# One transpose transfer for two heads' exponentials, a bfloat16 identity, more engine options and a new order in an attention and two-layer MoE kernel

## The chip, the cores and the metric

The kernel runs on one core of a Trainium2 chip. The metric is the device time of one launch in microseconds (us), lower is better. A profile of one execution of the kernel before is read below; its stretches are in us from the span's start.

## What is computed

The reference runs attention with a position bias and then two feed-forward layers, here called MoE 1 and MoE 2, on the result (batch 4, 8 heads, 576 positions, head width 64, model width 512, inner width 2048):

```python
scores = scale * np.matmul(q, k.transpose(0, 1, 3, 2))
x = (psi_rel / psi_i)[..., None]          # log1p distances
h = np.maximum(x @ w1 + b1, 0.0)
bias = h @ w2                             # one bias matrix for each head
scores = scores + bias.transpose(2, 0, 1)[None, :, :, :]
scores = scores - np.max(scores, axis=-1, keepdims=True)
attn = np.exp(scores)
attn = attn / (np.sum(attn, axis=-1, keepdims=True) + 1e-09)
attn_out = np.matmul(attn, v)             # then (tokens 2304, width 512)
r = np.maximum(x @ moe_w_in, 0.0)
x = (s * (r * r) + b) @ moe_w_out         # MoE 1
h = x @ moe2_w_in
out = (h - np.tanh(h)) @ moe2_w_out       # MoE 2
```

## The kernel before, in words

All products are made in half precision with a high and a low part (three products high-high, high-low, low-high), so most values are split into `hi` (a copy in float16) and `lo` (the remainder).

**The planner.** No order is written out by hand. Each piece of work is a task (`sc.add`) with the engines that may run it and a cost on each. While the program is built, class `Schedule` walks through the tasks in simulated time: of those that can start first it emits the one with the lowest priority number, which is a due time plus an entry of the table `SHIFT`. `COST` multiplies the costs by kind of task and engine, `XFER` the time and landing delay of transfers, `ENGINE` narrows the engines of a kind in one stage. Each engine then executes its own instructions in the emitted order. All transfers are issued from one queue, SP's, in order too. Buffers are rings: an instance of a ring with n slots can start only when the instance n places before it has been used up.

**The bias.** `bias_tasks` makes 36 strips Q: four hidden tiles (`hid`, on DVE, ACT, or POOL for Q < `QG`), a matmul (`pb`), two scaling copies into a tile of the ring `et` (`out`, on ACT or DVE), and a store to `btd` in DRAM. The heads load their bias rows `bi` from there.

**A unit.** 144 units stand for 144 heads' blocks of 128 query rows (with 64 rows left over, two heads share one). `unit_rest` does for each: add the bias and take the maximum (`ttr`, DVE, L1073), add a constant to the maximum (`mx_add`, L1081), the exponential into `e` (`ex`, ACT, L1087), its float16 copy (`hi`, L1097 on DVE or L1099 on ACT) and its remainder (`lo_a`, `lo_b`, L1104 on POOL or DVE) into one tile of the ring `hl` (3 slots), a transpose transfer of that tile's nine blocks of 128 columns into a tile of the ring `et` (4 slots, shared with the bias strips; L1119), and 14 matmuls with the values (`pv`, L1132 and L1138). Scores come from `qk` (L1041) into two PSUM slots `s`, which the exponential frees.

```python
def tr(_):
    nc.sync.dma_start_transpose(
        out=put(et, row_tile("et", F16).rearrange("p (n r) -> p n r", r=128)), in_=hl.tile
    )
t_tr[u] = sc.add({SP: (1.25, 1.4)}, tr, t_lo, d + 5 - 500, [et], [hl])
```

**The rest.** Four units make a group; `x_tasks` scales it, splits it (`xh`) and transposes it (L1217, L1220). MoE 1 runs in nine blocks of 256 tokens between the units: `ph` matmuls (L1573), `relu` and `square` on ACT (L1586, L1591), `hi` and `lo`, `po` matmuls (L1645). Its weights arrive as 64-bit numbers and are converted by three DVE passes (L1253, L1256, L1259), bounded by `norm_max` (a matmul `pm` with a 128 x 128 identity, L1341) and split (`w1_split`). When the last unit is done, `turn` changes the buffers, the weights of MoE 2 are converted and split, mostly on DVE, and 18 half blocks run through `in_product` (L2038, results `pa`, `pb`, copied by `copy`, L2057) and `out_product` (L2166, `acc`).

Of the kernel before, what the change touches and what calls it, by code (L numbers as in the profile page):

```python
# [31 lines left out]
COST = {
    "u.ex@act": 0.848, "u.hi@act": 0.904, "bias.lambda@act": 1.1, "f.relu@act": 0.952, "f.square@act": 1.15,
    "x.lambda@act": 1.2, "w.lambda@act": 1.13, "scan.sq@act": 1.17, "bias.out@act": 1.0315, "f.out@act": 1.1149,
    "w.square@act": 1.07, "k.hi@act": 1.15, "s.lambda@act": 1.09, "q.hi@act": 1.2, "v.hi@act": 1.14,
    "u.ttr@dve": 0.84944, "f.hi@dve": 1.152216, "u.hi@dve": 0.87312, "s.in_done@dve": 1.1143, "scan.add@dve":
    0.8125, "f.lambda@dve": 1.174, "s.out_done@dve": 1.662, "u.lo@pool": 0.9991, "f.lo@pool": 0.782085,
    "bias.lambda@pool": 1.0466, "u.qk@pe": 0.885, "u.pv@pe": 0.97, "u.tr@sp": 1.04, "x.lambda@sp": 1.083,
    "q.fn@sp": 1.36, "J.c@dve": 1.2701, "J.fn@dve": 1.12, "L.lambda@dve": 1.0069, "L.square@act": 0.919,
    "P.wsum@dve": 1.0042, "X.scales@dve": 0.7943, "X.sums@dve": 1.21, "X.xsum@dve": 1.1245, "bias.lambda@dve":  # L40
    1.0453, "bias.out@dve": 1.179, "f.norm@dve": 1.2446, "f.out@dve": 1.0696, "f.scales@dve": 0.4404,
    "k.hi@dve": 1.1296, "k.lambda@dve": 1.047, "q.hi@dve": 1.1098, "s.lambda@dve": 1.0224, "scan.lambda@dve":
    0.857, "v.hi@dve": 1.738, "v.lambda@dve": 1.0251, "w.lambda@dve": 0.993, ".begin@dve": 0.784, ".lambda@dve":
    1.116, "L.scales@dve": 0.961, "L.sums@dve": 0.868, "X.lambda@act": 1.021, "X.lambda@dve": 1.023,
    "q.lambda@dve": 1.026, "w.scale_out@dve": 0.859, "u.lo@act": 0.97, "u.lo_a@act": 0.97, "u.lo_b@act": 0.97,
    "u.lo@dve": 0.97, "u.lo_a@dve": 0.97, "u.lo_b@dve": 0.97, "u.lo_a@pool": 0.97, "u.lo_b@pool": 0.97,
    "f.lo@act": 0.85, "f.lo@dve": 0.85, "f.hi@act": 1.04, "f.hi@pool": 1.04, "u.hi@pool": 0.8, "u.ex@dve": 0.8,
    "u.ex@pool": 0.8, "u.ttr@act": 0.8, "u.ttr@pool": 0.8,
}
# [2277 lines left out]
```

## Time and the profile before

| | us |
|---|---|
| median of three runs | 1053.27 (1051.8 to 1054.85) |
| the profiled execution | 1057.96 |
| its span, first to last instruction | 1056.2 |
| PE busy in the span | 964.1 |
| DVE busy | 881.6 |
| ACT busy | 667.5 |
| POOL busy | 250.1 |

The profiled execution took 1.76 us more than its span and 4.69 us more than the median of the runs. The units run from about 40 to 572 us, the last block of MoE 1 ends at about 704 us, and the products of MoE 2 fill the rest. PE is TensorE's matmuls, PEld its weight loads, DVE is VectorE, ACT ScalarE, POOL GpSimd, SPq the queue from which transfers are issued. The granted clock (PEclk) is a share of the full 2.4 GHz; the other level, 1.2 GHz, shows as 0.5.

### The profile page before, as it was taken

To read this page: it belongs to the slowest core of one execution; us is meant where nothing else is said; L and a number is where in the kernel's file an instruction comes from. 1 tells how busy PE (TensorE), PEld (TensorE's weight loads), DVE (VectorE), ACT (ScalarE), POOL (GpSimd) and SP (SyncE) were. 2 spreads that over 40 slices of the span, in tenths; PEclk is the share of its full clock that TensorE was granted. 3 is DMA by queue.
4 is the path that set the end of the run, shared out by engine and by line. 5 is a ranking of instruction groups with operands and counts; after the bars stand their busy time and mean duration, and the time that the engine had idled before them with its cause. 6 is when DMAs were issued, how large, how long until landed. Compare 5 with 4: busy or idle time off the path is not lost.

```text
span 1056.2 us, 32450 instructions
## 1 busy us (share of the span) xinstructions
PE 964.1 (91%) x13486; PEld 833.2 (79%) x13486; DVE 881.6 (83%) x1918; ACT 667.5 (63%) x1307; POOL 250.1 (24%) x319
## 2 busy tenths in 40 slices
PE   5676678999988999999997999988999999999998
PEld 3233356778767788788886888878999999999998
DVE  6999899876568677786774889999999999999885
ACT  4797659749767565776853687766554555464452
POOL 6146437247542334455511000000000000000000
PEclk9767679899999999999999999998999999999999
DMA  9969995899999879999896904410001100100000
GB/s 341 398 227 216 311 236 119 184 200 252 245 197 230 168 179 176 201 188 207 171 180 104 397 21 138 148 36 12 32 23 32 52 23 22 42 22 23 22 22 22
DMA packets 261444, 153.66 MB, mean 145 GB/s; under 512 B 197680, under 2 KB 229552, under 8 KB 261296
## 3 DMA queue, kind: packets, MB, share of 16 engines
q1 hardware_dynamic: 261296, 151.59, 59.1%
q8 instruction: 105, 1.72, 0.7%
q14 instruction: 43, 0.35, 0.1%
HBM read 84.03 MB, written 20.33 MB: 99 GB/s over the span
## 4 chain that ended last, share of the span: by engine, by line
PE 43%; DVE 9%; ACT 3%; DMA 2%; issue 2%; POOL 1%; SPq 0%; DVEq 0%; ACTq 0%; POOLq 0%
PE acc L2166 14%; PE pa L2038 9%; PE pb L2038 7%; PE po L1645 5%; PE ph L1573 4%; PE po L2166 2%; DMA et<-hl 2%; DVE w2big L1852 2%; DVE w2big L618 1%; PE sp L1041 1%; DVE w1big L618 1%; ACT e L1087 1%; POOL hl L1104 1%; PE xp L1132 1%; DVE hr L1603 1%
## 5 line engine op out<-in xcount | busy, mean ns | idle before, releaser
L1645 PE MATMUL po<-hr,w1big 128*128 128x256 f16 x1728 | 202.9, 274 | 3.6 <-ACT x L1664 2.7
L1104 POOL TENSOR_TENSOR hl<-e,hl 128x64 f16<-128x64 f32 (+1 forms) x200 | 160.2, 818 | 184.9 <-ACT hl L1099 107.2
L1573 PEld LDWEIGHTS <-w1big 128*128 128x128 f16 x1728 | 166.9, 99 | 31.5 <-issue 10.6
L1645 PEld LDWEIGHTS <-w1big 128*128 128x128 f16 x1728 | 165.5, 98 | 26.5 <-issue 7.1
L2038 PEld LDWEIGHTS <-w2big 128*128 128x128 f16 x3024 | 175.2, 99 | 2.2 <-issue 2.1
L2166 PEld LDWEIGHTS <-w1big 128*128 128x128 f16 x3024 | 172.8, 98 | 0.0
L1087 ACT ACTIVATE e<-sp,mx 128x576 f32<-128x576 f32 x144 | 105.6, 735 | 70.3 <-POOL mx L1081 34.3
L1073 DVE CUSTOM_DVE_ANT_0 sp<-sp,bi 128x576 f32<-128x576 f32 x144 | 107.0, 772 | 20.2 <-PE sp L1041 16.2
L1573 PE MATMUL ph<-xt_own,w1big 128*128 128x256 f16 x960 | 113.1, 274 | 3.0 <-ACT r L1586 2.2
L1041 PE MATMUL sp<-ks,qs 64*128 64x288 f16 (+1 forms) x960 | 84.2, 296 | 25.8 <-ACT e L1087 24.8
L1573 PE MATMUL ph<-w1big 128*128 128x256 f16 x768 | 91.2, 276 | 3.3 <-ACT r L1586 2.6
L1041 PEld LDWEIGHTS <-qs 64*128 64x128 f16 (+1 forms) x960 | 48.7, 99 | 53.0 <-issue 42.2
L1132 PEld LDWEIGHTS <-et 128*128 128x128 f16 (+1 forms) x1440 | 54.7, 104 | 41.2 <-issue 21.5
L1132 PE MATMUL xp<-vp,et 128*128 128x64 f16 (+1 forms) x1440 | 65.4, 199 | 19.1 <-DMA et<-hl 11.7
L2166 PE MATMUL acc<-hr,w1big 128*128 128x128 f16 x1296 | 79.9, 219 | 0.0
L1099 ACT ACTIVATE hl<-e 128x576 f16<-128x576 f32 x96 | 64.7, 678 | 23.1 <-DMA et<-hl 20.2
L2166 PE MATMUL acc<-w2big,w1big 128*128 128x128 f16 x1296 | 79.0, 219 | 0.0
L1104 DVE TENSOR_TENSOR hl<-e,hl 128x512 f16<-128x512 f32 (+1 forms) x88 | 48.8, 572 | 15.9 <-ACT hl L1099 13.0
L2038 PE MATMUL pa<-w1big,w2big 128*128 128x128 f16 x960 | 59.9, 219 | 1.7 <-ACT w2big L2057 0.9
L1586 ACT ACTIVATE r<-ph 128x512 f32<-128x512 f32 x72 | 42.3, 590 | 25.8 <-PE ph L1573 21.3
L1591 ACT ACTIVATE r<-r,sq 128x512 f32<-128x512 f32 x72 | 51.2, 718 | 0.9
L2074 ACT ACTIVATE w1big<-w1big 128x512 f32<-128x512 f32 x34 | 21.3, 630 | 45.6 <-DVE w1big L2064 33.4
(229 smaller groups left out, 1757.7 us busy)
## 6 DMA issues: line engine op xcount, KB each, us to landing
bi<-btd SPq DMA_DIRECT2D x64, 288.0 KB, 4.1
w1big<-in_wout SPq DMA_DIRECT2D x12, 1024.0 KB, 6.0
btd<-et SPq DMA_DIRECT2D x36, 295.5 KB, 3.7
w1big<-in_win SPq DMA_DIRECT2D x8, 1024.0 KB, 9.7
w2big<-in_win SPq DMA_DIRECT2D x8, 1024.0 KB, 13.1
x2d<-x SPq DMA_DIRECT2D x36, 128.0 KB, 3.1
w1big<-x2d SPq DMA_DIRECT2D x36, 128.0 KB, 2.3
outT<-xt_own SPq DMA_DIRECT2D x18, 256.0 KB, 2.2
```

Source lines behind the costliest of these rows:

```text
L1041: nc.tensor.matmul(out=out, lhsT=qs.tile[64 * h:64 * h + 64, sq, p * r:p * r + r], rhs=ks.tile[64 * h:64 * h + 64, sk, half * HS:(half + 1 ...
L1073: nc.vector.tensor_tensor_reduce(out=st, in0=st, in1=bi.tile.rearrange("p (a b) -> p a b", a=2), scale=-1.0 / KAP, scalar=3.0e38, op0=ALU. ...
L1087: nc.scalar.activation(out=put(e, row_tile("e")).rearrange("p (a b) -> p a b", a=2), in_=sp.tile[:, :, 0:HS], func=AF.Exp, scale=-1.0, bia ...
L1099: nc.scalar.activation(out=h[:, 0:S], in_=e.tile, func=AF.Copy)
L1104: eng_of(eng).tensor_tensor(out=hl.tile[:, o:o + m], in0=e.tile[:, c:c + m], in1=hl.tile[:, c:c + m], op=ALU.subtract)
L1132: nc.tensor.matmul(out=xp[r0:r0 + r, o:o + 64], lhsT=et.tile[:, n, r0:r0 + r], rhs=vp.tile[:, 0, n % 5, 64 * h:64 * h + 64], start=n == 0, ...
L1573: nc.tensor.matmul(out=ph.tile[:, fi, :], lhsT=win_ap(1, sw, m, f), rhs=xa(sx, m), start=m == 0 and j == 0, stop=m == KM - 1 and j == 2,)
L1586: nc.scalar.activation(out=r.tile, in_=ph.tile, func=AF.Relu)
L1591: nc.scalar.activation(out=r.tile, in_=r.tile, func=AF.Square, scale=sq[:, fp // 4:fp // 4 + 1])
L1645: nc.tensor.matmul(out=po.tile[:, :NB1], lhsT=wout_ap(1, sw, f, c), rhs=rhl[f // 8][:, f % 8, sr, :], start=f == 0 and j == 0, stop=f == K ...
L2038: nc.tensor.matmul(out=bank.tile[:, f * HT:(f + 1) * HT], lhsT=w[:, sw, m, f * 128:(f + 1) * 128], rhs=xs[:, sx, m], start=p in (1, 2, 5) ...
L2166: nc.tensor.matmul(out=bank.tile[:, o + c * HT:o + (c + 1) * HT], lhsT=w[:, sw, f, c * 128:(c + 1) * 128], rhs=g[:, sx, f], start=new and ...
```

## The change

- Two units of a group (an even and an odd one) share one instance of `hl` and one of `et`, each twice as wide; both rings now have 2 slots. Their `hi` and `lo` fill the two halves, and one transfer transposes 18 blocks. It depends on the remainders of both units. `pv` of both units (moved into `unit_pv`) depends on it.
- Two bias strips (even and odd Q) share one instance of `et` in the same way; the odd strip's copies come after the even strip's.
- The identity and the column that multiplies it in `norm_max` become bfloat16.
- More options: `mx_add` on ACT; `relu` and the `copy` of MoE 2 on DVE; the hidden tiles on POOL for all strips (`QG` 36).
- `SHIFT` is replaced whole, `ENGINE` mostly, and many entries of `COST` and `XFER`: the planned `ex` goes from 0.78 x 0.848 to 0.78 x 1.0706, `hi` on ACT from 0.60 x 0.904 to 0.60 x 1.1865, on DVE from 0.42 x 0.873 to 0.42 x 1.249, `ttr` from 0.80 x 0.849 to 0.80 x 0.966. In the planner, POOL tasks without a port share no longer wait for DVE.
- In `ENGINE`, the tasks of the first 16 strips are narrowed: hidden tiles 0 to 7 to ACT or POOL, 8 to 15 to ACT, both sets of copies to ACT. `mx_add` is narrowed to DVE for units 0 to 11, 20 to 23, 36 to 39 and 80 to 95, to ACT for 40 to 47, to POOL for 112 to 127, and to two engines in most other stages (before: to POOL for units 12 to 15, 24 to 27 and 48 to 63). In MoE 2, `copy` and the `hi` splits go to DVE in half blocks 6, 10, 13, 16 and 17 (before: the splits in 5 and 13).

```diff
-SHARE0, QP, QA, SCU, QG = 21, 8, 16, 12, 7
+SHARE0, QP, QA, SCU, QG = 21, 8, 16, 12, 36
-    ROWS = dict(bi=4, e=2, hl=3, et=4)
+    ROWS = dict(bi=4, e=2, hl=2, et=2)
...
+        n = {"et": 2 * S + 32, "hl": 2 * S}.get(name, S)
+        t = row_p.tile([128, n], F32, tag=name, name=name, bufs=ROWS[name])
...
-    eye32 = const.tile([128, 128], F32, name="eye32")
+    eye16 = const.tile([128, 128], BF16, name="eye16")
...
-        ev = inst("et")
+        ev = ev_of[Q] = ev_of[Q - 1] if Q % 2 else inst("et")
+        eo = Q % 2 * (S + 16)
...
-        t_ev = [sc.add({ACT: 0.87, DVE: 0.80}, out, t_bmm[Q], d, [ev], [i])]
+        t_ev = [sc.add(
+            {ACT: 0.87, DVE: 0.80}, out, t_bmm[Q] + (t_evs[Q - 1] if Q % 2 else []), d, [] if Q % 2 else [ev], [i, ev]
+        )]
...
-        e, hl, et = inst("e"), inst("hl"), inst("et")
+        e = inst("e")
+        odd = k % 2
+        hl, et = hl_of[u], et_of[u] = (hl_of[u - 1], et_of[u - 1]) if odd else (inst("hl"), inst("et"))
+        h0 = odd * 2 * S
...
+            if eng == ACT:
+                nc.scalar.activation(out=m, in_=m, func=AF.Copy, bias=LN_E)
-        t_mx = sc.add({DVE: 0.16, POOL: 0.3}, mx_add, [t_ttr[u]], d + 1.5)
+        t_mx = sc.add({DVE: 0.16, POOL: 0.31, ACT: 0.2}, mx_add, [t_ttr[u]], d + 1.5)
...
+        if not odd:
+            return
...
-        t_tr[u] = sc.add({SP: (1.25, 1.4)}, tr, t_lo, d + 5 - 500, [et], [hl])
+        t_tr[u] = t_tr[u - 1] = sc.add({SP: (1.4, 2.8)}, tr, t_los[u - 1] + t_lo, d + 5 - 500, [et], [hl])
+        for v in (u - 1, u):
+            unit_pv(v)
...
-            nc.tensor.matmul(out=pm.tile, lhsT=m.to_broadcast([128, 128]), rhs=eye32, start=True, stop=True)
+            nc.tensor.matmul(out=pm.tile, lhsT=m.to_broadcast([128, 128]), rhs=eye16, start=True, stop=True)
...
-            tr = sc.add({ACT: 0.21 + 0.8e-3 * 2 * w}, relu, tp + [t_bs], ready - 400, [r], [ph])
+                if e == DVE:
+                    nc.vector.tensor_scalar(out=r.tile, in0=ph.tile, scalar1=0.0, scalar2=None, op0=ALU.max)
...
-                {ACT: 0.68}, lambda _: nc.scalar.activation(out=home(i), in_=bank.tile, func=AF.Copy, scale=ich),
+                {ACT: 0.68, DVE: 0.66}, lambda e: copy_scale(home(i), bank.tile, ich, e),
```

## Rows read from the trace of the kernel before

**Rows 1.** Busy time by stretch: engines' busy us (x instructions), PEclk, DMA share, GB/s
```profile
0.00:200.00 200.00, 140.10 (x1507) 84.81 (x1508) 179.98 (x370) 148.20 (x301) 93.49 (x81) 0.80 0.90 259
20.00:72.00 52.00, 34.06 (x223) 13.54 (x224) 51.40 (x99) 42.59 (x81) 17.34 (x8) 0.67 0.90 336
200.00:580.00 380.00, 362.77 (x4860) 301.57 (x4856) 268.10 (x739) 251.19 (x569) 156.60 (x239) 1.00 0.97 193
580.00:730.00 150.00, 139.06 (x1370) 124.78 (x1369) 139.02 (x225) 108.98 (x201) 0.00 (x0) 0.97 0.37 131
730.00:1050.00 320.00, 320.00 (x5725) 320.00 (x5723) 292.50 (x582) 159.14 (x240) 0.00 (x0) 1.00 0.09 27
```

**Rows 2.** The chain that ended last, in order of time: start us, length us, what
```profile
544.85 3.68 DMA et<-hl
...
553.95 2.87 DMA et<-hl
...
558.16 5.11 DMA et<-hl
...
721.13 5.28 PE pb L2038 x48
```

**Rows 3.** Waits of the whole span: us in total, times, longest us
```profile
ACT e L1087 <- POOL mx L1081: 34.3, 22, 3.1
...
PE sp L1041 <- ACT e L1087: 24.8, 30, 2.6
...
ACT hl L1099 <- DMA et<-hl: 20.2, 22, 2.5
...
ACT e L1087 <- DVE mx L1081: 19.4, 17, 3.8
...
PEld L1132 <- DMA et<-hl: 18.1, 17, 3.1
...
PE xp L1132 <- DMA et<-hl: 11.7, 11, 2.5
```

**Rows 4.** Instructions of lines L1119 and L1217: ns min/median/max, first and last start
```profile
L1119 SPq DMA_TRANSPOSE et<-hl x144: 1241/1350/4232, 66.6 to 566.1; - x144
L1217 SPq DMA_TRANSPOSE xt_own<-xh x16: 1189/1220/2143, 92.6 to 556.7; - x16
```

**Rows 5.** Transfers by line: count, median us from issue to landing (L1217's: 4 blocks)
```profile
btd<-et SPq DMA_DIRECT2D x36, 295.5 KB, 3.7
...
et<-hl SPq DMA_TRANSPOSE x144, 4.0
...
xt_own<-xh SPq DMA_TRANSPOSE x32, 3.1
```

**Rows 6.** Groups of instructions from 20 to 72 us: busy us, mean ns | idle before
```profile
L727 ACT ACTIVATE hr<-u_sb,cst_sb 128x416 f32<-128x416 f32 (+11 forms) x33 | 18.7, 633 | 0.0
L730 POOL TENSOR_SCALAR hr<-u_sb,cst_sb 128x480 f32<-128x480 f32 (+2 forms) x4 | 11.5, 2884 | 0.9 <-PE pb L761 0.9
L615 ACT ACTIVATE et<-pb,cst_sb 128x63 f32<-128x63 f32 (+14 forms) x15 | 6.6, 486 | 5.2 <-PE pb L761 5.2
L611 DVE TENSOR_SCALAR et<-pb,cst_sb 128x496 f32<-128x496 f32 (+9 forms) x10 | 4.8, 518 | 0.0
L613 POOL TENSOR_SCALAR w1big<-w1big,w_c 128x1024 f16<-128x1024 f32 x1 | 2.9, 2854 | 30.5 <-DMA btd<-et 30.5
L730 DVE TENSOR_SCALAR hr<-u_sb,cst_sb 128x448 f32<-128x448 f32 (+2 forms) x4 | 1.7, 446 | 0.0
```

**Rows 7.** Costliest groups of the whole span: busy us, mean ns | idle before
```profile
L1087 ACT ACTIVATE e<-sp,mx 128x576 f32<-128x576 f32 x144 | 105.6, 735 | 70.3 <-POOL mx L1081 34.3
L1073 DVE CUSTOM_DVE_ANT_0 sp<-sp,bi 128x576 f32<-128x576 f32 x144 | 107.0, 772 | 20.2 <-PE sp L1041 16.2
...
L1132 PE MATMUL xp<-vp,et 128*128 128x64 f16 (+1 forms) x1440 | 65.4, 199 | 19.1 <-DMA et<-hl 11.7
L1099 ACT ACTIVATE hl<-e 128x576 f16<-128x576 f32 x96 | 64.7, 678 | 23.1 <-DMA et<-hl 20.2
```

**Rows 8.** Instructions of lines L1341 and L2064: ns min/median/max, first and last start
```profile
L1341 PE MATMUL pm<-eye,wr x4: 421/488/582, 58.4 to 83.3; 128*128 128x128 f32 x4
L2064 DVE SCALAR_TENSOR_TENSOR w2big<-pb,cols,w2big x18: 740/746/752, 719.6 to 1027.1; 128x512 f32<-128x512 f32 x18
```

**Rows 9.** Busy time from 810 to 850 us, columns as in rows 1
```profile
810.00:850.00 40.00, 40.00 (x718) 40.00 (x716) 39.61 (x83) 18.24 (x28) 0.00 (x0) 1.00 0.11 36
```

**Rows 10.** Instructions of the tile et from 66 to 239 us, columns as in rows 4
```profile
L1119 SPq DMA_TRANSPOSE et<-hl x44: 1241/1324/4232, 66.6 to 236.1; - x44
...
L468 SPq DMA_DIRECT2D btd<-et x21: 319/517/1609, 71.5 to 238.9; - x21
```

More of the change, by code (lines that the diff above doesn't have):

```diff
@@ L30 @@
 WI0, WI1, WO0, WO1 = 27.23, 74.31, 71.56, 137.63
-AHEAD = 6.97
+AHEAD = 8.39
 COST = {
-    "u.ex@act": 0.848, "u.hi@act": 0.904, "bias.lambda@act": 1.1, "f.relu@act": 0.952, "f.square@act": 1.15,
+    "u.ex@act": 1.0706, "u.hi@act": 1.1865, "bias.lambda@act": 1.1, "f.relu@act": 0.952, "f.square@act": 1.15,
     "x.lambda@act": 1.2, "w.lambda@act": 1.13, "scan.sq@act": 1.17, "bias.out@act": 1.0315, "f.out@act": 1.1149,
     "w.square@act": 1.07, "k.hi@act": 1.15, "s.lambda@act": 1.09, "q.hi@act": 1.2, "v.hi@act": 1.14,
[L36 to L48, printed above, removed]
@@ new lines @@
+    "u.ttr@dve": 0.966238, "f.hi@dve": 1.118979, "u.hi@dve": 1.24908, "s.in_done@dve": 1.1143, "scan.add@dve":
+    1.0563, "f.lambda@dve": 1.3736, "s.out_done@dve": 1.662, "u.lo@pool": 1.0815, "f.lo@pool": 0.846492,
+    "u.qk@pe": 0.885, "u.pv@pe": 0.97, "u.tr@sp": 1.04, "x.lambda@sp": 1.083, "q.fn@sp": 1.36, "J.c@dve":
+    1.2701, "J.fn@dve": 1.12, "L.lambda@dve": 1.0069, "L.square@act": 0.919, "P.wsum@dve": 1.0042,
+    "X.scales@dve": 0.7943, "X.sums@dve": 1.21, "X.xsum@dve": 1.1245, "bias.lambda@dve": 1.0453, "bias.out@dve":
@@ new lines @@
+    1.179, "f.norm@dve": 1.2446, "f.out@dve": 1.0696, "f.scales@dve": 0.5065, "k.hi@dve": 1.412, "k.lambda@dve":
+    1.047, "q.hi@dve": 1.3318, "s.lambda@dve": 1.0224, "scan.lambda@dve": 0.9598, "v.hi@dve": 1.738,
+    "v.lambda@dve": 1.0251, "w.lambda@dve": 0.993, ".begin@dve": 0.784, ".lambda@dve": 1.116, "L.scales@dve":
+    0.961, "L.sums@dve": 0.868, "X.lambda@act": 1.021, "X.lambda@dve": 1.023, "q.lambda@dve": 1.026,
+    "w.scale_out@dve": 0.859, "u.lo_a@dve": 1.47, "u.lo@act": 1.05, "u.lo_a@act": 1.05, "u.lo_b@act": 1.05,
@@ L49 @@
+    "u.lo@dve": 1.05, "u.lo_b@dve": 1.05, "u.lo_a@pool": 1.05, "u.lo_b@pool": 1.05, "f.lo@act": 0.92,
+    "f.lo@dve": 0.92, "f.hi@act": 1.01, "f.hi@pool": 1.01, "u.hi@pool": 1.05, "u.ex@dve": 1.01, "u.ex@pool":
+    1.01, "u.ttr@act": 0.91, "u.ttr@pool": 0.91,
 }
 XFER = {
-    "bias.fn": (0.79893, 1.75), "f.fn": (1.5147, 1.23), "k.fn": (1.07019, 1.73), "q.fn": (1.05633, 1.81),
-    "scan.fn": (0.80982, 2.01), "u.fn": (1.21869, 1.21), "u.tr": (1.0197, 2.23), "v.fn": (0.97218, 2.27),
-    "w.fn": (0.91872, 2.03), "x.fn": (1.188, 1.54), "x.lambda": (0.81873, 1.51), "L.fn": (0.87714, 2.6), "J.fn":
@@ L54 @@
-    (0.33264, 1.52), "X.fn": (1.54341, 1.41), "o.fn": (0.8514, 0.99), ".fn": (0.78903, 1.4),
+    "bias.fn": (0.79893, 1.93), "f.fn": (1.5147, 1.41), "k.fn": (1.07019, 1.91), "q.fn": (1.05633, 1.99),
+    "scan.fn": (0.80982, 2.19), "u.fn": (1.21869, 0.67), "u.tr": (1.0197, 2.17), "v.fn": (0.97218, 2.45),
+    "w.fn": (0.91872, 2.21), "x.fn": (1.188, 1.72), "x.lambda": (0.81873, 2.71), "L.fn": (0.87714, 2.78),
+    "J.fn": (0.33264, 1.7), "X.fn": (1.54341, 1.59), "o.fn": (0.8514, 1.17), ".fn": (0.78903, 1.58),
@@ L267 @@
 class Schedule:
-    HOP = dict(pe=0.57, act=-0.03, dve=0.16, pool=0.37, turn=0.0)
+    HOP = dict(pe=0.57, act=-0.05, dve=0.12, pool=0.42, turn=0.0)
     LATE = dict(act=0.034, dve=0.034, pool=0.034)
@@ L286, in add @@
         only = ENGINE.get(t.key) or ONLY.get(kind)
+        if only is not None and not any(e in only for e in opts):
+            only = None
         t.opts = {}
@@ L290, in add @@
                 if isinstance(c, tuple):
-                    k, d = XFER.get(kind, (0.99, 1.79))
+                    k, d = XFER.get(kind, (0.99, 1.97))
                     t.opts[e] = (c[0] * 0.95 * COST.get(kind + "@" + e, 1.0), c[1] * k, d)
@@ L346, in forward @@
                         at = max(at, port["pool"] - self.LEAD)
-                    elif eng == "pool" and t.opts[eng] < self.LONG:
+                    elif eng == "pool" and t.share > 0.0 and t.opts[eng] < self.LONG:
                         at = max(at, port["dve"] - self.LEAD)
@@ L390, in forward @@
             else:
-                if eng == "pool" and cost < self.LONG or eng == "dve" and t.share > 0.0:
+                if t.share > 0.0 and (eng == "pool" and cost < self.LONG or eng == "dve"):
                     port[eng] = at + cost
@@ L684, in eye @@
         nc.gpsimd.affine_select(
-            out=eye32, in_=ones32, pattern=[[-1, 128]], compare_op=ALU.is_equal, fill=0.0, base=0, channel_multiplier=1,
+            out=eye16, in_=ones32, pattern=[[-1, 128]], compare_op=ALU.is_equal, fill=0.0, base=0, channel_multiplier=1,
         )
@@ L1057, in tile_kernel @@
     s_of, t_last = {}, [None]
+    hl_of, et_of, t_his, t_los = {}, {}, {}, {}
     def unit_rest(u):
@@ L1094, in hi @@
         def hi(eng):
-            h = put(hl, row_tile("hl", F16))
+            h = (hl.tile if odd else put(hl, row_tile("hl", F16)))[:, h0:h0 + S]
             if eng == DVE:
-                nc.vector.tensor_copy(out=h[:, 0:S], in_=e.tile)
+                nc.vector.tensor_copy(out=h, in_=e.tile)
             else:
-                nc.scalar.activation(out=h[:, 0:S], in_=e.tile, func=AF.Copy)
-        t_hi = sc.add({ACT: 0.60, DVE: 0.42}, hi, [t_exp[u]], d + 3, [hl], [e])
+                nc.scalar.activation(out=h, in_=e.tile, func=AF.Copy)
+        t_hi = t_his[u] = sc.add(
+            {ACT: 0.60, DVE: 0.42}, hi, [t_exp[u]] + ([t_his[u - 1]] if odd else []), d + 3, [] if odd else [hl], [e, hl]
+        )
         def lo(eng, part):
@@ L1104, in lo @@
             eng_of(eng).tensor_tensor(
-                out=hl.tile[:, o:o + m], in0=e.tile[:, c:c + m], in1=hl.tile[:, c:c + m], op=ALU.subtract
+                out=hl.tile[:, h0 + o:h0 + o + m], in0=e.tile[:, c:c + m], in1=hl.tile[:, h0 + c:h0 + c + m],
+                op=ALU.subtract,
             )
@@ L1121, in tr, with unit_pv @@
             )
-        t_tr[u] = sc.add({SP: (1.25, 1.4)}, tr, t_lo, d + 5 - 500, [et], [hl])
+        t_tr[u] = t_tr[u - 1] = sc.add({SP: (1.4, 2.8)}, tr, t_los[u - 1] + t_lo, d + 5 - 500, [et], [hl])
+        for v in (u - 1, u):
+            unit_pv(v)
+    def unit_pv(u):
+        sc.tag = f"u{u // 4 if u < 40 else 10 + u // 16}"
+        b, it, p, a, col = unit_of(u)
+        n, k = u // NP, u % NP
+        full = rows_of[it] == 128
+        et, vp, xp_i = et_of[u], vp_t[b, p], xp_of[n]
+        e0 = k % 2 * 9
         def pv(_):
@@ L1288, in w1_split @@
             sc.add(
-                {ACT: 1.04, DVE: 0.72, POOL: 3.0},
+                {ACT: 1.04, DVE: 0.72, POOL: 3.4},
                 lambda e, j=j: copy_scale(pr[:, 0, j * 1024:(j + 1) * 1024], w32_ap(i, j), c(), e), deps, prio,
@@ L1582, in moe1_in, with relu @@
             last = tp[-1:]
-            def relu(_, fp=fp, ph=ph, r=r):
+            def relu(e, fp=fp, ph=ph, r=r):
                 put(r, r_p.tile([128, 2, NB1], F32, tag="r", name="r")[:, :, :w])
-                nc.scalar.activation(out=r.tile, in_=ph.tile, func=AF.Relu)
-            tr = sc.add({ACT: 0.21 + 0.8e-3 * 2 * w}, relu, tp + [t_bs], ready - 400, [r], [ph])
+                if e == DVE:
+                    nc.vector.tensor_scalar(out=r.tile, in0=ph.tile, scalar1=0.0, scalar2=None, op0=ALU.max)
+                else:
+                    nc.scalar.activation(out=r.tile, in_=ph.tile, func=AF.Relu)
+            tr = sc.add(
+                {ACT: 0.21 + 0.8e-3 * 2 * w, DVE: 0.12 + 1.05e-3 * 2 * w}, relu, tp + [t_bs], ready - 400, [r], [ph],
+                share=0.0,
+            )
             def square(_, fp=fp, r=r):
```

48 lines of the change are left out of this document (26 added, 22 removed), and 272 rows, old and new, of tables (ENGINE, SHIFT).

## The prediction, on record before the changed kernel ran

> **What bounds the kernel now.** I read first the busy time by stretch [rows 1]. After 730 us PE is busy for 320.00 of 320 us at full clock: the products of MoE 2 run back to back, and nothing there can end earlier unless it starts earlier. Between 200 and 580 us PE lacks 380 - 362.8 = 17.2 us, between 580 and 730 us 10.9 us. The large hole is ahead of 200 us: PE lacks 59.9 us there, and its mean granted clock is 0.80. In that stretch DVE has 180.0 of 200 us, and from 20 to 72 us it has 51.4 of 52, while ACT has 42.6 and POOL 17.3: the start is bound by DVE. So 88.0 us of idle PE lie before 730 us, and time can be won only out of these and out of the half-speed clock of the start.
>
> Second, the chain that ended last [rows 2]: near the end of the units it passes through transposes of 3.68, 2.87 and 5.11 us, and from 721 us on it is PE alone. A transpose that lands late at the units' end is on the path.
>
> Third, the waits [rows 3]. PE waited 11.7 us for a transpose (11 times) and 24.8 us for an exponential that had yet to free its PSUM slot (30 times). The exponentials in turn waited 34.3 us for `mx_add` on POOL (22 times, 1.56 us each) and 19.4 us for `mx_add` on DVE (17 times, 1.14 us each). ACT waited 20.2 us for a free slot of `hl`, which a landed transpose frees.
>
> **The transfer of 18 blocks.** Issuing nine blocks takes 1.350 us at the median and 1.241 at least, four blocks 1.189 at least [rows 4]: five more blocks cost 0.05 us. Nine more on top of nine thus cost at least 0.09, in all 1.33 us; two issues in full are 2.70. I take 1.45, near the lower end, because the measured step is small. SP then spends 72 x 1.45 = 104 us instead of 144 x 1.35 = 194 on them, so transfers queued behind (bias rows, queries, stores, `x` transposes) leave earlier. From issue to landing nine blocks take 4.0 us and four 3.1 [rows 5], 0.18 us a block; 18 blocks then take 4.0 + 9 x 0.18 = 5.6 us. The upper bound is two after the other, 8.0; I take 5.6. A rule of the Trainium skill, DMA: Bandwidth & Descriptors, section Anatomy of one DMA, fits a fixed part of about 2.0 us and bytes over 436 GB/s (for another kind of queue); for 0.59 MB that estimate is 3.35 us, under even the measured 4.0 of nine blocks, so the trace doesn't agree, and by that rule the term for the end of the units below would be zero.
>
> What PE regains: the 11.7 us. Half of it I leave lost, as the first head of a pair now waits for the remainder of the second: -6, between 0 and -11.7. The new wait costs at least one unit's pitch, (566.1 - 66.6)/143 = 3.5 us [rows 4], plus 1.6 us of landing. Behind the waiting `pv` on PE stand the next `qk` and the MoE 1 matmuls; the planner emits `pv` later by that much, with those matmuls ahead of it, which are the cover from about 150 us on. If this cover is gone, 5.1 us are lost at that place. At the end of the units there is nothing left to cover: +1.6 (0 to +5.1). Behind the transfer on SP, in order, stand the next rows of bias; a transfer placed too early would hold them up by up to a pitch.
>
> The wider `hl` (four units' places instead of three) removes part of ACT's 20.2 us. ACT has 251.2 of 380 us there [rows 1], so I count nothing for it; if ACT had no other idle time it would be worth the 20.2.
>
> **Bias work away from DVE.** From 20 to 72 us DVE made 10 copies (4.8 us) and 4 hidden tiles (1.7) of the first 16 strips [rows 6]. The change forbids both to DVE: 6.5 us off the bound engine. ACT takes at most 4 x 0.633 + 10 x 0.486 = 7.4 us more and would stand at 42.6 + 7.4 = 50.0, above DVE's 44.9. An even share of both engines is (51.4 + 42.6)/2 = 47.0, that is -5.0 against 52; POOL, which sat idle for 30.5 us before its weight copy [rows 6], can take hidden tiles at 2.88 us each. I take -4, between 0 (ACT becomes the bound) and -6.5.
>
> **`mx_add`.** A wait behind POOL was 0.42 us longer than one behind DVE; 22 x 0.42 = 9.2 us of ACT [rows 3]. Of ACT's two waits (53.7 us) PE felt 24.8, so the share is 0.46 and the bound -4.3. Only some stages leave POOL: -2, between 0 and -4.3.
>
> **The order.** The planner's old cost of an exponential is 0.78 x 0.848 = 0.66 us and the new one 0.84; the trace has 0.735 and a read of the accumulator besides. `hi` on ACT: 0.54 before, 0.71 now, measured 0.678; `ttr` 0.68, 0.77, measured 0.772 [rows 7]. So the new order is planned with durations that fit this chip. Of the 88.0 us of idle PE, 36.5 are the two waits already counted; of the other 51.5 I give a better order an eighth: -6, between -26 (half) and +13 (a worse order; a quarter). No row shows it: it is the softest term.
>
> **At nothing.** The bfloat16 `pm`: its two calls show four matmuls of 0.488 us [rows 8], so each call takes two passes; at most one of each falls away, 0 to -1.0, and DVE's conversions hide it. `copy` on DVE: 20 copies at about 0.75, the nearest row being a DVE operation on PSUM [rows 8], 15 us, covered by DVE's 320 - 292.5 = 27.5 idle us [rows 1]; but half block 6 lies near 721 + 6 x 18.3 = 831 us (18 half blocks from 721 to 1050), where DVE has 39.61 of 40 us [rows 9]. There 4 x 0.75 = 3.0 us of copies, and as much again of splits, come in while half block 5 and preparations leave DVE; without that cover PE waits up to 6 us. `relu` on DVE in block 5: eight operations while DVE has 268 of 380 us.
>
> **Sum.** -6 + 1.6 - 4 - 2 - 6 = -16.4 us. The span 1056.2 becomes 1039.8 and the profiled execution, with 1.76 us around the span, 1041.6. That execution lay 4.69 us above the median of the runs, so the forecast against the median 1053.27 is 1037 us. With all lower ends the sum would be -49.5 (-11.7 - 6.5 - 4.3 - 26 - 1.0), with the upper ends +24 (5.1 + 13 + 6).
>
> **Rivals.**
> 1. *Hidden anyway.* PE is at 95% from 200 to 580 us [rows 1]; a freer SP queue then buys nothing, and the order is only another one: -4 + 1.6 - 2 gives 1049, with another few us lost 1053. Against it: PE did wait for transposes.
> 2. *The `et` ring bounds the start* (slower). Its two slots serve unit pairs and strip pairs in turn, and are handed out in order. From 66 to 239 us there are 44 transposes and 21 strip stores [rows 10]. A `pv` takes 14 x 65.4/1440 = 0.64 us [rows 7], a strip about 1.0 for its copies and 3.7 to land [rows 5]. Before: (44 x 4.64 + 21 x 4.7)/4 = 76 of 173 us per slot. After, with strips 173/21 = 8.2 us apart: (22 x 6.9 + 10.5 x 12.9)/2 = 144 us; with a landing of 8.0 us it is (22 x 9.3 + 10.5 x 12.9)/2 = 170. It decides from a landing of about 8 us, or when strips of a pair lie more than some 10 us apart. If only nine tenths of a slot's time can be used, 170 become 189: +16, less 6 of the other terms, 1063 us. Against it: strips of a pair can be placed side by side.
> 3. *POOL gets in DVE's way.* If twelve more hidden tiles of 2.88 us ran on POOL [rows 6], and each held up a DVE operation by half its length, DVE lost 12 x 1.44 = 17 us, the whole gain: 1054. SBUF — State Buffer of the Trainium skill, section Who interferes with whom, states that the second of two such instructions blocks until the first ends; by that rule this rival would follow for operations that share the port.
>
> **Chances.** The forecast 0.55 (its own range 1022 to 1046), a still larger gain 0.06, rival 1 0.18, rival 2 0.14, rival 3 and a full DVE near 830 us 0.07. Less than 0.3%, about 3 us, can't be told from no change in this kernel. Faster holds the first two and a third of rival 1: 0.67. The same: another third and some of rival 3: 0.09. Slower: the remainder, 0.24. The range 1017 to 1062 leaves out the largest gains and the upper half of rival 2.
>
> **What would show it.** 72 transposes on SP near 1.45 us that land in about 5.6; DVE without bias work from 20 to 72 us, with ACT near 48; fewer PE waits for `et` and for `ex`; the first `acc` near 710 instead of 726 us, with PE still full behind it. The prediction is wrong if ACT instead of DVE bounds the start, if copies of strips (`et`) wait for landings, if the landing is near 8 us, or if PE has holes near 830 us.

## The result, and the profile after

The changed kernel takes **1063.53 us** (median of 4 runs, 1062.66 to 1064.26), the kernel before 1054.06 in the same session (1051.8 to 1055.28): ratio **1.0092**, 95% interval 1.0071 to 1.0112. It is slower; the forecast of 1037 us had the wrong sign, and the time lies above its range.

Busy time by stretch of the kernel after (engines' busy us and instructions, PEclk, DMA share, GB/s), against [rows 1]:

```profile
0.00:200.00 200.00, 141.52 (x1520) 83.34 (x1521) 173.55 (x357) 157.65 (x322) 102.95 (x86) 0.85 0.91 263
20.00:72.00 52.00, 34.92 (x230) 14.49 (x226) 48.88 (x83) 46.79 (x93) 22.22 (x14) 0.77 0.92 330
200.00:580.00 380.00, 359.53 (x4822) 297.73 (x4820) 268.93 (x729) 254.67 (x590) 148.18 (x206) 0.99 0.92 189
580.00:730.00 150.00, 136.19 (x1341) 121.76 (x1339) 143.28 (x242) 102.05 (x184) 0.00 (x0) 0.98 0.37 133
730.00:1050.00 320.00, 319.88 (x5681) 319.75 (x5679) 305.10 (x608) 140.95 (x212) 0.00 (x0) 0.99 0.09 27
```

PE's idle time is what is left of each stretch. Up to 200 us it is 58.5 us (59.9 in [rows 1]), to 580 us 20.5 (17.2), to 730 us 13.8 (10.9), and behind that 0.1. So 1.4 us are won at the start and 6.2 lost in the units and at the handover to MoE 2: 4.8 us more idle time, and the span is 5.3 us longer (1061.5 against 1056.2). The other part of the 9.5 us between the medians can't be read from the two traces, since the profiled execution of before lay above its median and that of after just under it.

The transfer, line L1145 (ns min/median/max, first and last start) and its row among the transfers (median us from issue to landing), against [rows 4, 5]:

```profile
L1145 SPq DMA_TRANSPOSE et<-hl x72: 2429/3314/6565, 68.6 to 565.0; - x72
```
```profile
et<-hl SPq DMA_TRANSPOSE x72, 5.7
```

The landing is the forecast one, 5.7 us. The issue isn't: 2.43 us at least and 3.31 at the median. Summed over the records, 72 issues held SP for 253.7 us, and the 144 of before for 240.1. SP has won nothing.

Waits of the whole span (us in total, times, longest), against [rows 3]:

```profile
ACT e L1107 <- POOL mx L1101: 22.8, 14, 3.0
PE sp L1054 <- ACT e L1107: 22.0, 30, 2.8
...
ACT e L1107 <- DVE mx L1101: 18.4, 12, 4.4
PEld L1168 <- DMA et<-hl: 17.3, 14, 3.5
ACT hl L1119 <- DMA et<-hl: 16.8, 14, 3.3
...
ACT mx L1099 <- DVE mx L1090: 15.8, 17, 2.1
...
PE xp L1168 <- DMA et<-hl: 12.2, 9, 3.4
```

PE still waits 12.2 us for transposes (11.7 before). The exponentials wait 11.5 us less for `mx_add` on POOL, but ACT, which now makes some of these itself, waits 15.8 us for their maxima. PE's wait for a slot `s` is 2.8 us shorter over the whole span, and none of that lies between 200 and 580 us, where it is 6.6 us before and 7.5 after:

```profile
PE sp L1041 <- ACT e L1087: 6.6, 10, 2.3
```
```profile
PE sp L1054 <- ACT e L1107: 7.5, 13, 1.0
```

In the chain that ended last (start, length, what) the larger transposes stand in the middle of the units, and an issue on SP is itself a piece of the chain:

```profile
269.86 9.32 DMA et<-hl
...
300.86 5.00 DMA et<-hl
309.54 2.86 SPq L1145
...
322.61 10.88 DMA et<-hl x2
336.76 14.42 DMA et<-hl x2
...
428.93 6.00 DMA et<-hl
...
547.25 5.41 DMA et<-hl
```

The chain of before can be followed back only to 422 us, so the two can't be compared ahead of that. Behind it, up to 580 us, transposes are 11.4 us of the chain after and 20.3 of the chain before.

The first `acc` starts at 727.7 us (726.2 before). Between 695 and 745 us the products of MoE 2 wait for conversions, among them `acc` once it has started (the first three lines below). Before has its longest wait there ahead of the first `acc`, at `psum` (the last line), 1.7 us for conversions, and none of `acc`:

```profile
PE acc L2208 <- ACT hr L622: 2.3, 1, 2.3
PE pa L2080 <- ACT w1big L622: 2.2, 1, 2.2
PE pb L2080 <- ACT w2big L622: 2.1, 1, 2.1
```
```profile
PE psum L695 <- DVE w2big L2064: 3.9, 1, 3.9
```

### The profile page after: what moved, and what is told of

It is laid out like the page before. It is cut to its first block, busy times and chain, and to the rows that moved or that the text cites. A ratio compares the mean times of both kernels' runs of the same rounds, so it can differ in the third digit from the quotient of the medians.

```text
span 1061.5 us, 32168 instructions
## 1 busy us (share of the span) xinstructions
PE 964.5 (91%) x13484; PEld 829.8 (78%) x13484; DVE 897.1 (85%) x1946; ACT 656.0 (62%) x1307; POOL 251.1 (24%) x291
## 4 chain that ended last, share of the span: by engine, by line
PE 53%; DVE 20%; DMA 11%; issue 6%; ACT 5%; POOL 2%; SPq 2%; DVEq 0%; ACTq 0%; POOLq 0%
PE acc L2208 13%; PE ph L1609 9%; PE po L1687 8%; PE pa L2080 8%; PE pb L2080 6%; DMA et<-hl 6%; PE sp L1054 3%; DVE sp L1090 2%; PE xp L1168 2%; PE po L2208 2%; DVE w1big L625 2%; ACT e L1107 1%; DVE w2big L1292 1%; DVE w2big L625 1%; DMA w1big<-in_qT 1%
## 5 line engine op out<-in xcount | busy, mean ns | idle before, releaser
L1126 POOL TENSOR_TENSOR hl<-e,hl 128x64 f16<-128x64 f32 (+1 forms) x169 | 143.7, 870 | 148.9 <-ACT hl L1119 108.3
L1107 ACT ACTIVATE e<-sp,mx 128x576 f32<-128x576 f32 x144 | 105.4, 734 | 55.7 <-POOL mx L1101 22.8
L1119 ACT ACTIVATE hl<-e 128x576 f16<-128x576 f32 x106 | 69.8, 677 | 17.4 <-DMA et<-hl 16.8
L1126 DVE TENSOR_TENSOR hl<-e,hl 128x64 f16<-128x64 f32 (+1 forms) x119 | 62.8, 547 | 18.0 <-ACT hl L1119 15.8
L1168 PE MATMUL xp<-vp,et 128*128 128x64 f16 (+1 forms) x1440 | 63.6, 197 | 12.8 <-DMA et<-hl 12.2
L1168 PEld LDWEIGHTS <-et 128*128 128x128 f16 (+1 forms) x1440 | 52.3, 103 | 25.5 <-DMA et<-hl 17.3
L2116 ACT ACTIVATE w1big<-w1big 128x512 f32<-128x512 f32 x34 | 21.4, 629 | 61.8 <-DVE w1big L2106 34.3
L2080 PE MATMUL pa<-w2big 128*128 128x128 f16 x768 | 48.1, 219 | 0.0
```

Source lines behind the costliest of these rows:

```text
L1107: nc.scalar.activation(out=put(e, row_tile("e")).rearrange("p (a b) -> p a b", a=2), in_=sp.tile[:, :, 0:HS], func=AF.Exp, scale=-1.0, bia ...
L1119: nc.scalar.activation(out=h, in_=e.tile, func=AF.Copy)
L1126: eng_of(eng).tensor_tensor(out=hl.tile[:, h0 + o:h0 + o + m], in0=e.tile[:, c:c + m], in1=hl.tile[:, h0 + c:h0 + c + m], op=ALU.subtract,)
L1168: nc.tensor.matmul(out=xp[r0:r0 + r, o:o + 64], lhsT=et.tile[:, e0 + n, r0:r0 + r], rhs=vp.tile[:, 0, n % 5, 64 * h:64 * h + 64], start=n ...
L2080: nc.tensor.matmul(out=bank.tile[:, f * HT:(f + 1) * HT], lhsT=w[:, sw, m, f * 128:(f + 1) * 128], rhs=xs[:, sx, m], start=p in (1, 2, 5) ...
```

## The experiments

The runs of the kernel before that each session had beside it are what the ratios stand against. "Order kept" means that the planner's order is that of the kernel named, and only what a task emits is edited.

**1. One transfer or two (e1, order of after kept).**

```diff
-dma_start_transpose(out=et[18 blocks], in_=hl.tile)
+for i in range(2):
+    dma_start_transpose(out=t[:, 9*i:9*i+9], in_=hl.tile[:, 2*S*i:2*S*i+2*S])
```

> The changed kernel, order and buffers kept, but the transfer of 18 blocks is issued as two transfers of nine blocks one behind the other. Theory A (issue is paid per block: the 18 blocks held SP 2.43 us at least, twice the 1.24 us of nine blocks before): two issues of about 1.24 us at least, the same SP time within a tenth, and a time within 4 us of the changed kernel's 1063.5. Rival (one large transfer is itself worse: it holds SP in one piece and lands late): the first nine blocks don't help, as both heads wait for the whole, but SP is held less, and the time falls by 4 us or more, to 1059 or less.

1064.77 us, ratio 1.0073 [1.005, 1.0096]: as the kernel after. 144 issues at a median of 1.384 us hold SP for 242.8 us in all, the 72 of after at 3.314 for 253.7. Theory A holds: one large transfer is worth nothing against two of nine.

**2. Pairs and tables taken apart, planned anew (e2, e3, e4).** e2 is after without pairs, with the new tables and engine options; e3 has the pairs with the tables and options of before; e4 is after with the planner told of the true issue time:

```diff
-{SP: (1.4, 2.8)}
+{SP: (2.6, 2.8)}
```

> The changed kernel without the pairs: each unit and each bias strip has its own slot and transfer again (rings of 3 and 4), all else as changed, the new tables included, and the planner makes its order from them. Theory P (the pairs cost the time: no issue time saved, a wait for the second head): 1054 or less. Theory T (the new tables and narrowed engines cost it): 1060 or more.

> The kernel before with the pairs alone (two units and two strips share a slot, one transfer of 18 blocks, bfloat16 identity) and its own old tables and options. Theory P (the pairs cost the time): 1063 or more. Theory T (the new tables cost it): 1050 to 1057.

> The changed kernel with one number changed in the planner: the issue of a pair's transfer is planned with 2.6 us of SP instead of 1.4, near the 2.43 us that the trace shows at least. Theory I (the order is bad since it was planned with half the issue time): 1057 or less. Rival (the planned issue time hardly matters, or an order not searched for is worse): 1061 or more.

1075.84 (1.0177 [1.0147, 1.0207]), 1098.34 (1.0389 [1.0362, 1.0416]) and 1088.87 (1.0294 [1.0262, 1.0326]). All three are slower than both kernels, and they contradict each other: e2 falls in the range of theory T (the tables cost the time), e3 in that of theory P (the pairs do). In each the planner made an order that its table of `SHIFT` had not been searched for; that had to be priced first (e8).

**3. The price of an order that was not searched for (e8).** The kernel before, with one cost of the planner changed by 0.1 us and nothing else:

```diff
-t_tr[u] = sc.add({SP: (1.25, 1.4)}, tr, t_lo,
+t_tr[u] = sc.add({SP: (1.35, 1.4)}, tr, t_lo,
```

> The kernel before with one number changed in the planner: the planned issue of a transpose is 1.35 us, the median that the trace shows, instead of 1.25. The order is made anew from the same table that was searched for the old number. Theory O (an order that wasn't searched for costs one to three per cent whatever is changed): 1064 or more, as in the runs with exchanged tables. Rival (the planner's input hardly matters): within 3 us of the kernel before.

1078.54, ratio 1.0208 [1.018, 1.0235]. The same work, in another order: 2% slower. So e2 to e4 can't tell pairs from tables.

**4. The first head's blocks earlier (e6, order of after kept).** Two transfers of nine; the first one is issued right behind the first head's remainder, in 39 of the 72 pairs where its slot was free by then.

> The changed kernel, all engines' orders kept, but the transfer is made in two of nine blocks, and for 39 of the 72 pairs the first is issued at the place where the first head's remainder is emitted, without waiting for the second head (where a slot of et was free at that place). Theory W (the first head's wait for the second, and the late landing, cost the time): 1058 or less, with fewer PE waits for et. Rival (the wait is covered; the loss lies in the order of the other engines): 1061 to 1067.

1064.2, ratio 1.0075 [1.0053, 1.0097]. PE's waits for transposes nearly vanish, and ACT's for a slot of `hl` fall from 16.8 to 9.7 us:

```profile
ACT hl L1132 <- DMA et<-hl: 9.7, 11, 2.4
...
PEld L1197 <- DMA et<-hl: 2.7, 4, 1.0
...
PE xp L1197 <- DMA et<-hl: 0.8, 2, 0.5
```

and the time stays. From 200 to 580 us its waits show where PE stands instead: for exponentials, 9.4 us against 7.5 in the kernel after, and for keys that ACT converts late, as ACT waits for their load.

```profile
PE sp L1065 <- ACT e L1120: 9.4, 11, 4.2
PE sp L1065 <- ACT ks L622: 5.5, 1, 5.5
```
```profile
ACT ks L622 <- DMA kst<-in_kT: 7.8, 2, 7.6
```

**5. Half the blocks (e7, e10; order of after kept).** e7 transfers nine of the 18 blocks in one transfer, e10 five and four in two. The other nine blocks are left out, so the output is not the reference's:

```diff
+t = put(et, ...)
+dma_start_transpose(out=t[:, 0:9], in_=hl.tile[:, 0:2*S])        # e7
+for o, n in ((0, 5), (5, 4)):                                    # e10
+    dma_start_transpose(out=t[:, o:o+n], in_=hl.tile[:, 128*o:128*(o+n)])
-e0 = k % 2 * 9
+e0 = 0
```

> The changed kernel, order kept, but only the first nine of the 18 blocks are transferred, and both heads' products with the values read them (the second head's transposed exponentials are left out). So a pair costs SP about 1.24 to 1.35 us, near the 1.45 us that the prediction took, and half of the transposed bytes. Theory S (the mis-sized issue and transfer time is what turned the gain into a loss): 1052 or less, more than 10 us under the changed kernel. Rival (SP and the transfers are covered; the order of the other engines sets the time): 1058 to 1064.

> The changed kernel, order kept; as in the run with nine of the 18 blocks the second head's transposed exponentials are left out, but the nine blocks go in two transfers of five and four, so that SP is held for about 2 x 1.19 = 2.4 us as by 18 blocks while the DMA engines move half the bytes. Theory S1 (SP's issue time is the cost): 1058 or more. Theory S2 (the moved blocks are the cost: the DMA engines' time and the later landing): 1050 or less, near the 1046 of one transfer of nine. Between: both.

1046.43 (0.9909 [0.9887, 0.993]) and 1048.73 (0.9915 [0.9894, 0.9936]): 17 and 15 us under the kernel after (1.8% by the ratios). The transfer's row in e7 and in e10, and the stretch from 200 to 580 us in each:

```profile
L1146 SPq DMA_TRANSPOSE et<-hl x72: 1241/1312/3062, 68.9 to 550.6; - x72
```
```profile
L1147 SPq DMA_TRANSPOSE et<-hl x144: 1188/1222/3991, 68.6 to 553.7; - x144
```
```profile
200.00:580.00 380.00, 367.19 (x4939) 306.71 (x4936) 281.38 (x750) 261.85 (x606) 148.43 (x206) 1.00 0.70 158
```
```profile
200.00:580.00 380.00, 366.27 (x4929) 305.49 (x4927) 280.63 (x746) 261.13 (x606) 149.07 (x207) 1.00 0.71 156
```

e10 holds SP twice as often as e7 (144 issues, 192.1 us in all, against 72 and 117.5 us) and gains as much. So it is the moved blocks that bind, not SP's time: DMA engines are busy for 0.70 or 0.71 of the stretch instead of 0.92, and PE has 7 us more. With fewer blocks a transfer also lands earlier (3.7 us in e7 and 3.1 in e10 instead of 5.7); the DMA engines' time and the earlier landing aren't told apart here.

**6. The issue by itself (e9).** Only transfers of 1 to 18 blocks, six times a size, and rows of nine and of 18 blocks; nothing of the reference is computed. The single transfers were meant to run alone. The emitted order put some between others up to about 90 us; of 8 to 18 blocks, five of the six ran one at a time.

> A kernel that computes nothing of the reference: it transposes 1, 2, 4, 6, 8, 9, 10, 12, 14, 16 and 18 blocks six times each, each transfer alone on the chip (a small DVE copy reads its end before the next starts), then twelve transfers of nine blocks and six of 18 with nothing between them. Theory A (issue is a floor of about 1.2 us, and beyond about nine blocks it is paid per block): SP 1.2 us up to nine blocks, about 1.35 for ten, 1.6 for twelve, 2.43 for 18, and the rows of nine and of 18 take the same time in all. Rival (a step at some size, or the 2.43 us is only a full queue): 18 blocks alone are issued in about 1.3 us.

The instructions of its line of single transfers and, last, of its two rows (ns min/median/max):

```profile
L425 SPq DMA_TRANSPOSE one1x<-src x6: 1163/1213/1590, 3.3 to 30.0; - x6
...
L425 SPq DMA_TRANSPOSE one4x<-src x6: 1212/1223/1910, 5.8 to 75.4; - x6
...
L425 SPq DMA_TRANSPOSE one9x<-src x6: 1242/1286/1408, 9.8 to 129.6; - x6
...
L425 SPq DMA_TRANSPOSE one16x<-src x6: 1317/1806/2519, 18.8 to 211.2; - x6
L425 SPq DMA_TRANSPOSE one18x<-src x6: 2397/2690/2770, 23.1 to 235.4; - x6
```
```profile
L429 SPq DMA_TRANSPOSE rowof9x<-src x12: 1317/1365/1420, 27.2 to 49.3; - x12
```
```profile
L434 SPq DMA_TRANSPOSE rowof18x<-src x6: 2487/2762/2773, 50.7 to 69.9; - x6
```

The least duration rises from 1.163 us for one block to 1.317 for 16, some 0.01 us a block, and then stands at 2.397 for 18: a step, about the price of a second issue. The medians leave the least durations sooner: 1.340 at 10 blocks, 1.434 at 12, 1.520 at 14. Neither expectation came out whole. The rival had a step, but 18 blocks at 1.3 us; theory A had 2.43 for 18 and, for the rows, one time for both, and there the twelve transfers of nine held SP for 16.3 us in all and the six of 18 for 16.3 too. The landing went from 2.3 us (1 block) over 3.2 (9) to 4.6 (18).

**7. Relief of SP by another way (e11, e12; orders kept).** The loads of the bias rows are issued from ACT's queue, in the kernel after (e11) and in before (e12):

```diff
-t_bi[u] = load(lambda: put(bi, row_tile("bi")), bias_rows(...), ...)
+t_bi[u] = load(lambda: put(bi, row_tile("bi")), bias_rows(...), ..., q=adma)   # adma: nc.scalar.dma_start
```

> The changed kernel, order kept, but the 80 loads of bias rows are issued from ACT's queue instead of SP's (about 40 us of SP's time between 48 and 544 us). Theory S1 (SP's issue time is the cost): 1058 or less. Theory S2 (the DMA engines' time is the cost, which stays the same): 1061 to 1067; above that if the issues hold up ACT.

> The kernel before, order kept, with the same 80 loads issued from ACT's queue. Theory S1 (SP's issue time costs this kernel too): 3 us or more under the kernel before. Theory S2: within 3 us of it, or slower if the issues hold up ACT.

1072.23 (1.0145 [1.0115, 1.0175]) and 1071.67 (1.0126 [1.0101, 1.0152]): slower in both, against both expectations of theory S1. The 80 issues held ACT's queue for 33.5 us in e11 and 35.0 in e12, and the rows landed 4.7 us after their issue at the median, instead of 3.9 in the kernels before and after. Which of the two costs the time isn't told apart, so these runs say little of what a freer SP queue would be worth by itself.

**8. Orders carried over task by task (e13, e14).** The planner is replaced by a list: of the tasks that are ready, the one that stands first in the other kernel's order is emitted, on that kernel's engine. e13 is the kernel after in the order of before, e14 the kernel after without its pairs in the order of after.

```diff
-at, t = min((c for c in cand if c[0] <= lim), key=lambda c: (c[1].prio, c[1].seq))
+t = next(t for t in ready if free(t))   # ready: sorted by place in the given order
```

> The kernel after, with every engine's order and every choice of engine taken task by task from the kernel before; only what the pairs need is put otherwise: one transfer of 18 blocks where before has the second head's transfer, and the two pv of a pair at the place where before has the second head's, 2 us later by the planner's time. Theory O (the pairs cost nothing by themselves, the loss of 0.9% is the new order): 1052 to 1059, a ratio of 0.998 to 1.004. Theory P (the pairs cost by themselves, later landing and later pv, and the new order holds part of that back): 1064 or more, at least as slow as the kernel after. Theory G (the pairs gain and the new order loses it): under 1050.

> The kernel after without pairs: nine blocks a transfer, the slots of before, but every engine's order and every choice of engine of the kernel after; the first head's transfer stands right behind its own remainder, the second head's where after has the pair's. Theory O: 1060 to 1066, as the kernel after, since the order is the same and pairs cost nothing. Theory P: faster than the kernel after by 4 us or more, 1059 or less. Theory G: slower than the kernel after, 1068 or more.

1111.57 (1.0501 [1.048, 1.0522]) and 1107.77 (1.0463 [1.0443, 1.0484]): 5% slower either way. By its number e13 would speak for theory P (pairs cost), and e14 for theory G (pairs gain), so one contradicts the other: an order fits the transfers it was searched with, and neither run tells what pairs cost.

**9. The order of MoE 2 exchanged (e15, e16).** The 1098 tasks of MoE 2 take the other kernel's order and engines; all else is kept.

> The kernel after, with the order and the engines of the tasks of MoE 2 (preparation of its inputs, first products, second products: 1098 tasks) taken from the kernel before; the places in the order that such tasks have are the same, all else is the order of the kernel after. Theory T (the new order of these tasks loses the 3.8 us behind the first acc): 1058 to 1061, from the first acc to the end 330 us instead of 333.8. Rival (what stands ahead of these tasks sets it: they come 1 to 2 us later and the order fits only what it was searched with): 1062 to 1068.

> The mirror of the last: the kernel before, with the order and the engines of MoE 2's tasks taken from the kernel after. Theory T: 1056 to 1059, some 4 us slower than before, from the first acc to the end near 334 us. Rival: as before within 1.5 us, or slower by more than 6 because the order doesn't fit.

e15: 1071.54 (1.0129 [1.0106, 1.0151]), the rival's direction and beyond its range. e16: 1059.44 (1.0031 [1.0015, 1.0048]), just above theory T's range, some 3 us slower than before by the ratio. The stretch from 580 to 730 us of e16 and of e15, and e16 behind 730 us:

```profile
580.00:730.00 150.00, 135.80 (x1353) 122.25 (x1351) 136.14 (x222) 106.83 (x196) 0.00 (x0) 0.97 0.37 130
```
```profile
580.00:730.00 150.00, 136.18 (x1319) 121.76 (x1317) 134.57 (x218) 97.71 (x178) 0.00 (x0) 0.97 0.38 133
```
```profile
730.00:1050.00 320.00, 320.00 (x5724) 320.00 (x5722) 294.86 (x589) 154.81 (x233) 0.00 (x0) 1.00 0.09 27
```

In e16 PE is full behind 730 us, and from the first `acc` to the end it takes 329.9 us, as before (330.0) and not the 334 of theory T. Its loss lies ahead of that: from 580 to 730 us PE lacks 14.2 us, as much as in the kernel after (13.8) and 3.3 more than in before (10.9). So MoE 2's new order, put into the kernel before, brings a loss of this size at the handover with it. The reverse doesn't hold: in e15 the old order leaves the 13.8 us as they are and loses another 3.9 behind 730 us.

**10. Both orders with the same transfers (e17, order of before kept).** The transfers of e10 in the kernel before: five blocks for even heads, four for odd ones.

```diff
+nb = 5 - k % 2
-out=put(et, ...), in_=hl.tile
+out=t[:, 0:nb], in_=hl.tile[:, 0:128*nb]
-lhsT=et.tile[:, n, r0:r0 + r]
+lhsT=et.tile[:, n % nb, r0:r0 + r]
```

> The kernel before, order kept, with each unit's transfer cut to five blocks (even heads) or four (odd heads); pv reads these again in place of the other blocks, so half of the transposed exponentials are left out, as in the kernel after with five and four blocks (1048.73, ratio 0.9915), in the same number of transfers of the same sizes. Theory O (the 0.9% of the kernel after is its order): before gains as much as after did, some 15 us, and ends near 1040, a ratio of 0.980 to 0.986, 0.9% under that kernel. Theory P (the 0.9% comes of the transfers of pairs): both end alike, a ratio of 0.989 to 0.994. If before isn't bound by moved blocks: 1.000.

1039.31, ratio 0.9841 [0.9816, 0.9866], as theory O expected: some 17 us less than before. Its transfer and its stretch from 200 to 580 us:

```profile
L1121 SPq DMA_TRANSPOSE et<-hl x144: 1188/1206/2677, 66.4 to 551.5; - x144
```
```profile
200.00:580.00 380.00, 371.95 (x4978) 311.80 (x4976) 279.17 (x750) 259.32 (x586) 157.26 (x238) 1.00 0.74 163
```

With the same blocks in as many transfers of the same sizes the kernel after stands at 0.9915 and before at 0.9841: 0.75% between them, with intervals that don't meet, nearly all of the 0.92% between the kernels themselves. What after loses is not in its large transfers. e10 still has the other parts of the change, though: the pairs' shared slots, the wait of a pair's `pv` for both heads, the new engine options and the order planned with them. e17 doesn't tell these apart.

## Why the prediction was wrong

**The step that failed first is the issue of 18 blocks at 1.45 us.** It measured 2.43 at least and 3.31 at the median, over the upper bound of 2.70; by itself, in e9, it is 2.69 at the median, just that bound. The step from four to nine blocks, 0.05 us, was carried on to 18; e9 shows a jump between 16 and 18 and, in rows, no saving at all. The saving was also worked out from medians, 194 us for 144 issues, while their records sum to 240.1: the long ones, up to 4.2 us [rows 4], belong to the same queue. So SP's 90 us were never there: 253.7 us after, 240.1 before. By e7 and e10 they would have bought little: 75 us more of SP's time left the ratio where it was (0.9909 and 0.9915).

**The term of -6 for PE's waits was wrong beyond that.** PE's waits for transposes stayed (12.2 us); and e6, which took nearly all of them away, ended at the same time, with 5.5 us of PE waiting behind a load of keys instead. A wait for one transfer was counted as time that comes back once that transfer is earlier; with DMA engines busy for 0.92 to 0.97 of the stretch, e6 shows another transfer late instead. Only fewer blocks bought time, 15 to 18 us for half of them (e7, e10, e17), and pairs move as many blocks as before. The prediction read the DMA share in [rows 1] and made no use of it. Which transfer binds at which place isn't settled by these runs.

**The landing of 5.6 us was right** (5.7). The last matmul of `pv` started 1.2 us later (572.6 against 571.4), near the +1.6 for the end of the units. That may be luck: in e10 and e17, whose transfers are alike, the same place differs by 2.2 us (559.0 and 556.8).

**The bias work went as forecast, and its -4 was mis-sized.** DVE made no copy of strips before 76.7 us; from 20 to 72 us DVE has 48.9 us, 2.5 less than before where 6.5 were counted, and ACT 46.8, where the prediction had ACT near 48. The first MoE 1 product nevertheless came at 155.5 us instead of 153.5, and PE's idle time ahead of 200 us fell by 1.4 us. DVE's relief was real and the start doesn't end earlier by it.

**`mx_add`, -2, isn't borne out.** The waits behind POOL fell from 34.3 to 22.8 us, 10.0 us of it from 200 to 580 us. But PE's wait for a slot didn't fall there (6.6 us before, 7.5 after), and ACT has 15.8 us of new waits for the maxima to which it now adds the constant itself. Ahead of 200 us PE's wait fell by 3.7 us, which is part of the start's 1.4. So the 2.8 us of the whole span are near the forecast size by luck. The share of 0.46 was worked out over the whole span; 18.2 of the 24.8 us of PE's wait lie ahead of 200 us, where only 3.5 of the 34.3 us behind POOL do.

**The order, -6 with bounds of -26 and +13, is the other term that failed.** It was called the softest; by what the other terms leave, it had the wrong sign. The other terms as read from the trace (0 for the transfer, +1.2 for the end, -1.4 for the start, 0 for `mx_add` from 200 us on) sum to -0.2 us, and the span came out at +5.3. So some +5.5 us are left, inside the bounds of this term, for the order and for what no term names. e17 against e10 gives 0.75% or 8 us with like transfers, again for the order together with the pairs' slots and waits and the new options. That it is the order among these is not shown. The argument for a gain, that the new planner costs fit the measured durations, has e8 and e4 against it: a truer cost in the planner made a slower kernel. The order is one that was searched, and not one that follows from the costs. Where in the order it lies stays open. In e10 and e17 unit 36 starts its `pv` at 229.2 and 218.6 us, unit 72 at 364.7 and 369.1, unit 108 at 464.2 and 463.6, the first `acc` comes at 715.1 and 708.7, and the spans are 1047.6 and 1038.6: lost at the start, regained by the middle of the units, lost again from there on, most of it between the last `pv` and the first `acc` and behind that. MoE 2's order taken by itself cost before a third of the 0.92% (e16), at the handover.

**At nothing.** `pm` fell from four matmuls of 0.488 us to two of 0.230, 1.5 us less of PE and over the bound of 1.0; no gain of the time can be laid to it. The copies on DVE did no harm near 830 us: PE has no hole behind 730 us worth naming (0.1 us), though DVE has 305.1 us there instead of 292.5.

**The rivals.** "Hidden anyway" has a reason that e7 and e10 bear out, a freer SP buys little, but in the kernel after SP wasn't freer, and its times of 1049 and 1053 are 10 to 15 us too low. The `et` ring didn't set the time: the start came out 1.4 us better in PE's idle time, and the late unit 36 (227.6 against 220.0) had been made good by unit 72 (376.4 against 379.6). POOL in DVE's way: DVE was less busy up to 200 us, 173.6 against 180.0, which speaks against it; it wasn't tried by itself.

## What to carry to other kernels

Before a transfer is made larger to save its issue, measure the issue at the new size, and read the queue's time as a sum, not as count times median. Where the DMA share of a stretch is near full, as in this one, a wait for a transfer may not be worth its length: ask whether the change moves fewer bytes, and try the bound by moving half of them. An order that was searched is a part of the kernel worth some per cent (2.1% in e8), so a change that plans it anew is judged by experiments that keep one order and edit what it emits.

## What the runs showed of the hardware

The issue of a DMA transpose on SP has a step: 1.16 to 1.32 us at least for 1 to 16 blocks of 128 x 128 two-byte values, 2.40 for 18 (e9). With the next transfer right behind, nine blocks take 1.365 us and 18 take 2.762 at the median, so in a row the two sizes cost the same per block. The landing of single transfers grows by (4.6 - 2.3)/17 = 0.135 us a block, and a block is 32.8 KB, so about 242 GB/s; from nine blocks to 18 alone it is (4.6 - 3.2)/9 = 0.156 us, 211 GB/s. The Trainium skill, DMA: Bandwidth & Descriptors, section Latency and other measured facts, states 261 GB/s for a DMA transpose with a non-contiguous middle dimension, measured on one kernel, and 350 to 400 for the contiguous case. e9 lies below both, nearer to the first; which case its transfers are, no run shows.
